# The third block's query load moved ahead of eight weight copies, and an order of its own for the last second-layer steps

## The chip, the cores and the metric

The kernel runs on one core of a Trainium2 chip. The metric is the device time of one execution in microseconds (us). Three runs of the kernel before gave 1104.61, 1104.78 and 1104.95 us; the median is 1104.78.

## The reference

Attention through 49 agents, then two feed-forward layers, on 12,480 tokens of width 128 with 2,048 hidden units, all in float32:

```python
a2k = sm(agents, k)            # softmax over the 12480 keys
agent_v = a2k @ v              # 49 x 128
q2a = sm(q, agents)            # softmax over the 49 agents
x = q2a @ agent_v              # 12480 x 128
h = x @ w_in                   # first layer
g = where(h >= 1, h, where(h <= -1, 0, (h + 1)**2 / 4));  x = g @ w_out
h = x @ w_in                   # second layer, own weights
g = s * max(h, 0)**2 + b;      out = g @ w_out
```

## The kernel before

**Tiling.** The tokens are cut into 25 blocks (`widths`, line 99): 256, then 23 times 512, then 448. A block goes through each layer in eight steps of 256 hidden units, so a layer has 200 steps, 0 to 199; steps 192 to 199 belong to the last block. Every float32 operand of the large products is held as a high and a low part, so a product takes several matmuls.

**One step.** In layer 1: the hidden product (`H`, lines 589 and 621, on PE), relu and square (`R`, `S`, ACT, lines 651 and 657), the cap (`M`, DVE, line 661), the high part `gh` (`c`, line 670 on ACT or 672 on DVE), the low part `gl` (`L`, DVE, line 677), and six output matmuls into the accumulator `y` (`O`, line 716), of which the third and the sixth need `gl`. In layer 2 the same without the cap, in small letters: `h` (line 602), `r`, `t`, `g` (tokens `G` and `C`), `l`, and `o` into the accumulator `o`. From step 189 on `g` is always on DVE. A finished `y` is split on ACT and DVE (`Y`, `y`, lines 735 and 738) before layer 2 can use it; a finished `o` is scaled by DVE into `osb` (`Z`, line 742) and stored. There is one `y` and one `o` buffer, and three `h` buffers.

**Prologue and ramp.** The prologue decodes the weights, forms the agents' values, and multiplies them into the first layer's weights (`awh`, `awl`). The ramp (`RAMP`, line 78) is a written list for steps 0 to 13. The token `q2` in it computes the scores of the third block's queries on PE (line 169), with its softmax in the tokens `z2.0` to `z2.9`. From the third block on layer 1 uses repacked weights `awm` and `awx` that `fill_rows` (line 607) copies from `awh` and `awl` with eight DMAs (lines 613, 614, 616).

**The DMA queue.** Every DMA is issued by SP, in the order of the program. The program gives the DMAs eight completion counters in turn, so that SP also waits, before a DMA, until the eighth one before it has landed. `load_q` (line 155) loads a block's queries into one of two buffers.

**The steady part.** `steady` (line 767) goes through the steps two at a time (`n0` = 14, 16, ...). Layer 2 runs 11 steps behind layer 1, and the output matmuls run two steps behind their `h`. For each `n0` the table `PAIR` (line 88) says in which order each engine takes its tokens; tokens that have no work any more are left out. From `n0` = 200 on layer 1 has only `O` of steps 198 and 199, the low part of step 199 and the split of the last `y` left; the rest is layer 2's steps from 187 to 199. Each engine works strictly through its own list.

Of the kernel before, what the change touches and what calls it, by code (L numbers as in the profile page):

```python
# [18 lines left out]
def kernel(  # L19
# [40 lines left out]

    SEQ = (
# [12 lines left out]
        "v11 v12 D1 q1"  # L76
    )
    RAMP = (
# [9 lines left out]
    PAIR = {  # L88
        "PE": "H0 h0 O0 o0 q0 O1 p1 p0 h1 q1 o1".split(),
        "ACT": "t0 P0 Y0 R0 R1 Q0 S0 S1 G0 r0 P1 Y1 t1 r1 Q1 G1".split(),  # L90
        "DVE": "L0 y0 C0 C1 Z1 F0 M0 M1 l0 Z0 c0 y1 c1 L1 l1 F1".split(),
    }
    QS, QT, DX = 7, 5, 1
    MASK_H = 0x7FFFFE00
# [60 lines left out]
    def load_q(t):  # L155
        if t >= NB:
            return
        t0, w = blocks[t]
        q_t[t] = qp.tile([P, TB], F32, tag="q", name=f"q{t}")
        nc.sync.dma_start(out=q_t[t][:, :w], in_=qT[:, t0:t0 + w])  # L160
# [162 lines left out]
    def prologue():  # L323
        with ExitStack() as pctx:
            pro = pctx.enter_context(tc.tile_pool(name="pro", bufs=1))
            dec = pctx.enter_context(tc.tile_pool(name="dec", bufs=1))
            wi1h = pro.tile([P, DFF], F32R, name="wi1h")
            wi1l = pro.tile([P, DFF], F32R, name="wi1l")
            agents_values(pro, dec, wi1h, wi1l)

    def agents_values(pro, dec, wi1h, wi1l):
# [239 lines left out]
        steps = {p: decode(dec, *pieces[p[0]], p) for p in WORD}  # L571
        for token in SEQ.split():
            kind, _, arg = token.partition(".")
# [9 lines left out]
    NS = NB * JP  # L583
# [23 lines left out]
    def fill_rows():  # L607

        extra["m"] = late.tile([P, DFF], F32R, name="awm")
        extra["x"] = late.tile([P, DFF // 4], F32R, name="awx")  # L610
        m, x, h, l = (w.bitcast(F32) for w in (extra["m"], extra["x"], awh, awl))
        for i, r in enumerate((0, LO)):
            nc.sync.dma_start(out=m[r:r + NA], in_=h[r:r + NA])
            nc.sync.dma_start(out=m[r + NA:r + NA + X1], in_=l[i * X1:(i + 1) * X1])
        for g in range(P // RG):
            nc.sync.dma_start(  # L616
                out=x[g * RG:g * RG + XL].rearrange("p (q m) -> p q m", m=P),
                in_=l[XN:NA].rearrange("p (q g m) -> p q g m", g=4, m=P)[:, :, g, :],
            )
# [64 lines left out]
    def GH(layer, n):  # L684
        if layer == 1:
            return PAT1[n] if n < len(PAT1) else "0"
        return PAT2[n % len(PAT2)] if n < NS - TL else "0"
# [79 lines left out]
    def steady():  # L767
# [20 lines left out]
            fillers.extend(later.pop(0))  # L788

        for n0 in range(NR, NS + D + D2 + 2, 2):  # L790
            for e, tokens in PAIR.items():
                for token in tokens:
                    c, n = token[0], n0 + int(token[1])
                    m, j, t = n - D, n % JP, n // JP
                    a, b = n < NS, 0 <= m < NS

                    def slot(key):

                        slots.append(key)
                        return [slots[-4]] if len(slots) > 3 else []  # L800

                    def add(key, deps, fn, *args):
                        lists[e].append((key, deps, fn, args))

                    if c == "H" and a and n == n0:
                        add(("H", n), slot(("M", n)) + slot(("M", n + 1)), first, n)
                    elif c == "O" and n - 2 < NS:
                        k = n - 2
                        add(("O", k), [("L", k), ("y", k // JP - 1)], O, 1, k)
                    elif c == "h" and b:  # L810
                        add(("h", m), slot(("r", m)) + [("y", m // JP)], H, 2, m)
                    elif c == "o" and 0 <= m - 2 < NS:
                        k = m - 2
                        add(("o", k), [("l", k), ("Z", k // JP - 1)], O, 2, k)
                    elif c == "q" and j == QS and t + 2 < NB:
                        add(("q", t + 2), slot(("Q", t + 2)), scores, t + 2)
                    elif c == "p" and t > 1 and j == QT and t + 1 < NB:
                        add(("p", t + 1), slot(("P", t + 1)) + [("F", n - 1, 1), ("Q", t + 1)], q_transpose, t + 1)
                    elif c == "Q" and j == QS and t + 2 < NB:
                        add(("Q", t + 2), [("q", t + 2)], scores_copy)  # L820
                    elif c == "P" and t > 1 and j == QT and t + 1 < NB:
                        add(("P", t + 1), [("p", t + 1)], q_evac)
                    elif c == "R" and a:
                        add(("R", n), [("H", n), ("H", n - 1), ("L", n - XB)], relu, 1, n)
                    elif c == "S" and a:
                        add(("S", n), [("R", n)], square, 1, n)
                    elif c == "M" and a:
                        add(("M", n), [("S", n)], cap, n)
                    elif c == "c" and a:
                        add(("c", n), [("M", n), ("O", n - GR)], hi, 1, n, False)  # L830
                    elif c == "L" and n - 1 < NS:
                        add(("L", n - 1), [("c", n - 1), ("O", n - 1 - GR)], lo, 1, n - 1)
                    elif c == "r" and 0 <= m < NS - 1:
                        add(("r", m), [("h", m), ("l", m - XB)], relu, 2, m)
                    elif c == "r" and m == NS - 1:
                        add(("r", m), [("h", m), ("l", m - XB), ("o", m - GR)], last_step, True)
                    elif c == "t" and 0 <= m - 1 < NS - 1:
                        add(("t", m - 1), [("r", m - 1)], square, 2, m - 1)
                    elif c in "GC" and 0 <= m - 1 < NS - 1 and (c == "G") == (GH(2, m - 1) == "1"):
                        add(("g", m - 1), [("t", m - 1), ("o", m - 1 - GR)], hi, 2, m - 1, c == "G")  # L840
                    elif c == "l" and 0 <= m - 1 < NS - 1:
                        add(("l", m - 1), [("g", m - 1), ("o", m - 1 - GR)], lo, 2, m - 1)
                    elif c == "l" and m - 1 == NS - 1:
                        add(("l", m - 1), [("r", m - 1)], last_step, False)
                    elif c == "Y" and (n - 2) % JP == JP - 1 and n - 2 < NS:
                        add(("Y", (n - 2) // JP), [("O", n - 2)], evac, 1, "h")
                    elif c == "y" and (n - 2) % JP == JP - 1 and n - 2 < NS:
                        add(("y", (n - 2) // JP), [("Y", (n - 2) // JP)], evac, 1, "l")
                    elif c == "Z" and 0 <= m - 2 < NS and (m - 2) % JP == JP - 1:
                        add(("Z", (m - 2) // JP), [("o", m - 2)], evac, 2, "")  # L850
                    elif c == "F":
                        for x in range(2):
                            add(("F", n, x), [], fill)
# [10 lines left out]
    with tc.manual_schedule():  # L864
        prologue()
        late = ctx.enter_context(tc.tile_pool(name="late", bufs=1))
        fill_rows()
        ramp()
        fillers.append(lambda: nc.vector.tensor_scalar_mul(bcol, bcol, b_sb[:, 0:1]))
        steady()  # L870
# [35 lines left out]
```

## Time and profile before

| | |
|---|---|
| median of three runs | 1104.78 us (1104.61 to 1104.95) |
| profiled execution | 1106.68 us, of which the span of the profile is 1104.9 us |
| PE busy | 1072.0 us, 97% of the span |
| ACT busy | 969.9 us, 88% |
| DVE busy | 964.8 us, 87% |
| chain that ended last | PE 89%, DVE 5%, ACT 2%, DMA 1%, SP's queue 1% |

PE is the tensor engine's matmul side, DVE the vector engine, ACT the scalar engine, SPq the queue of SP. Busy shares are means over stages with different limits; the chain names what each moment waited for.

### The profile page before, as it was taken

To read this page: it belongs to the slowest core of one execution; us is meant where nothing else is said; L and a number is where in the kernel's file an instruction comes from. 1 tells how busy PE (TensorE), PEld (TensorE's weight loads), DVE (VectorE), ACT (ScalarE), POOL (GpSimd) and SP (SyncE) were. 2 spreads that over 40 slices of the span, in tenths; PEclk is the share of its full clock that TensorE was granted. 3 is DMA by queue.
4 is the path that set the end of the run, shared out by engine and by line. 5 is a ranking of instruction groups with operands and counts; after the bars stand their busy time and mean duration, and the time that the engine had idled before them with its cause. 6 is when DMAs were issued, how large, how long until landed. Compare 5 with 4: busy or idle time off the path is not lost.

```text
span 1104.9 us, 13492 instructions
## 1 busy us (share of the span) xinstructions
PE 1072.0 (97%) x5050; PEld 823.4 (75%) x5050; DVE 964.8 (87%) x1194; ACT 969.9 (88%) x1132; POOL 0.8 (0%) x7
## 2 busy tenths in 40 slices
PE   6887999999999999999999999999999999999997
PEld 2676777777777777777777777777777777777776
DVE  8887889889889889889889889889889889889875
ACT  6876899889889889889889989989989989989974
POOL 0000000000000000000000000000000000000000
PEclk9898999999999999999999999999999999999999
DMA  9920000000000000000000000000000000000000
GB/s 351 394 79 23 19 23 24 4 28 24 4 28 25 3 28 25 3 27 26 3 27 26 3 27 26 2 27 27 1 28 27 1 27 27 1 18 18 1 10 18
DMA packets 19973, 41.01 MB, mean 37 GB/s; under 512 B 2638, under 2 KB 7976, under 8 KB 19268
## 3 DMA queue, kind: packets, MB, share of 16 engines
q1 hardware_dynamic: 19908, 40.15, 10.6%
q8 instruction: 40, 0.66, 0.3%
q14 instruction: 25, 0.20, 0.1%
HBM read 27.58 MB, written 6.39 MB: 31 GB/s over the span
## 4 chain that ended last, share of the span: by engine, by line
PE 89%; DVE 5%; ACT 2%; DMA 1%; SPq 1%; issue 1%; DVEq 0%
PE h L602 26%; PE o L716 24%; PE y L716 23%; PE h L632 7%; PE h L638 4%; PE qs L169 2%; DVE gl L677 1%; DMA k<-in_kT 1%; DVE x L661 1%; PE tp L212 1%; PE av L457 1%; ACT x L657 1%; SPq L616 1%; DVE gh L672 1%; DVE mxs L414 1%
## 5 line engine op out<-in xcount | busy, mean ns | idle before, releaser
L677 DVE TENSOR_TENSOR gl<-x,gh 128x1024 fp32r<-128x1024 f32 (+2 forms) x399 | 469.4, 1193 | 20.0 <-ACT gh L670 19.8
L657 ACT ACTIVATE x<-x 128x1024 f32<-128x1024 f32 (+2 forms) x399 | 404.4, 1043 | 1.9
L661 DVE SCALAR_TENSOR_TENSOR x<-h,x 128x1024 f32<-128x1024 f32 (+2 forms) x200 | 230.5, 1192 | 77.0 <-ACT x L657 76.4
L653 ACT ACTIVATE x<-h 128x1024 f32<-128x1024 f32 (+2 forms) x199 | 201.3, 1012 | 59.6 <-PE h L602 59.6
L651 ACT ACTIVATE x<-h 128x1024 f32<-128x1024 f32 (+2 forms) x200 | 190.0, 1005 | 2.9 <-DVE gl L677 1.0
L672 DVE CAST gh<-x 128x1024 fp32r<-128x1024 f32 (+2 forms) x251 | 164.0, 678 | 15.4 <-ACT x L657 15.2
L602 PE MATMUL h<-yh,wi2h 128*128 128x512 f32 (+2 forms) x400 | 166.7, 417 | 0.9 <-DVE x L661 0.9
L716 PE MATMUL o<-gl,wo2h 128*128 128x512 f32 (+2 forms) x400 | 157.9, 395 | 5.2 <-DVE gl L677 5.2
L716 PE MATMUL o<-gh,wo2h 128*128 128x512 f32 (+2 forms) x400 | 157.7, 394 | 1.9 <-DVE osb L742 1.8
L716 PE MATMUL y<-gl,wo1h 128*128 128x512 f32 (+2 forms) x400 | 156.6, 391 | 1.3 <-DVE gl L677 1.3
L716 PE MATMUL y<-gh,wo1h 128*128 128x512 f32 (+2 forms) x400 | 156.2, 391 | 0.1
L716 PE MATMUL y<-gh,wo1l 128*128 128x512 f32 (+2 forms) x400 | 156.2, 390 | 0.0
L716 PE MATMUL o<-gh,wo2l 128*128 128x512 f32 (+2 forms) x400 | 155.6, 389 | 0.0
L602 PE MATMUL h<-yh,wi2l 128*128 128x512 f32 (+2 forms) x400 | 155.5, 389 | 0.0
L602 PE MATMUL h<-yl,wi2h 128*128 128x512 f32 (+2 forms) x400 | 155.4, 389 | 0.0
L670 ACT ACTIVATE gh<-x 128x1024 fp32r<-128x1024 f32 (+1 forms) x148 | 152.2, 1030 | 0.9 <-DVE x L661 0.8
L602 PEld LDWEIGHTS h<-yh,wi2h 128*128 128x128 f32 x400 | 75.0, 187 | 36.7 <-issue 17.0
L632 PE MATMUL h<-pt,awm 128*128 128x512 f32 (+1 forms) x368 | 99.2, 391 | 0.0
L716 PEld LDWEIGHTS o<-gl,wo2h 128*128 128x128 f32 x400 | 75.0, 188 | 28.3 <-DVE gl L677 12.2
L716 PEld LDWEIGHTS y<-gl,wo1h 128*128 128x128 f32 x400 | 75.6, 189 | 19.7 <-DVE gl L677 2.8
L716 PEld LDWEIGHTS o<-gh,wo2h 128*128 128x128 f32 x400 | 75.2, 188 | 18.8 <-DVE osb L742 2.1
L716 PEld LDWEIGHTS y<-gh,wo1h 128*128 128x128 f32 x400 | 75.6, 189 | 17.3 <-ACT gh L670 0.3
(114 smaller groups left out, 909.8 us busy)
## 6 DMA issues: line engine op xcount, KB each, us to landing
k<-in_kT SPq DMA_DIRECT2D x12, 512.0 KB, 12.7
v<-in_v_main SPq DMA_DIRECT2D x12, 512.0 KB, 8.5
q<-in_qT SPq DMA_DIRECT2D x23, 256.0 KB, 4.9
out_T<-osb SPq DMA_DIRECT2D x23, 256.0 KB, 2.1
wu<-in_w_in SPq DMA_DIRECT2D x4, 1024.0 KB
px<-pt SPq DMA_DIRECT2D x88, 38.0 KB
wu<-in_w_out SPq DMA_DIRECT2D x3, 1024.0 KB
pt<-pt SPq DMA_DIRECT2D x44, 30.0 KB
```

What stands on the lines that cost most here:

```text
L169: nc.tensor.matmul(out=scv[:, i, :], lhsT=qt[:, c0:c0 + P], rhs=aT, start=True, stop=True)
L602: nc.tensor.matmul(out=h[:, i, :w], lhsT=a[:, sl], rhs=r, start=(m == 0), stop=(m == len(ops) - 1))
L632: nc.tensor.matmul(out=out[g], lhsT=awm[:, c * P:(c + 1) * P], rhs=pt_t[t][:, :w], start=True, stop=False)
L638: nc.tensor.matmul(out=out[g], lhsT=awx[r, q], rhs=px_t[t][r, :w], start=False, stop=True)
L651: nc.scalar.activation(out=x, in_=h, func=ACTF.Relu, scale=0.5, bias=0.5)
L653: nc.scalar.activation(out=x, in_=h, func=ACTF.Relu)
L657: nc.scalar.activation(out=x, in_=x, func=ACTF.Square)
L661: nc.vector.scalar_tensor_tensor(out=x, in0=h, scalar=1.0, in1=x, op0=ALU.max, op1=ALU.min)
L670: nc.scalar.activation(out=a, in_=x, func=ACTF.Copy)
L672: nc.vector.tensor_copy(out=a, in_=x)
L677: nc.vector.tensor_tensor(out=b, in0=x, in1=a.bitcast(F32), op=ALU.subtract)
L716: nc.tensor.matmul(out=o[:, :w], lhsT=l[:, c, :], rhs=r[:, i, :w], start=(c == 0 and m == 0), stop=(c == KF - 1 and m == 2),)
```

## The change

The diff, without the unchanged parts of the tables:

```diff
     RAMP = (
-        "u2 H0 q1 R0 H1 S0 z1.0 M0 R1 z1.1 H2 g0 ...
+        "H0 q1 R0 H1 S0 z1.0 M0 R1 z1.1 H2 g0 ...
...
+    TAIL = {
+        "PE": "H0 O0 h0 o0 O1 h1 o1".split(),
+        "ACT": "Y0 R0 S0 t0 G0 r0 Y1 R1 S1 t1 G1 r1 P0 P1 Q0 Q1".split(),
+        "DVE": "C0 l0 L0 M0 y0 Z0 c0 F0 C1 l1 L1 M1 y1 Z1 c1 F1".split(),
+    }
...
         for n0 in range(NR, NS + D + D2 + 2, 2):
-            for e, tokens in PAIR.items():
+            for e, tokens in (PAIR if n0 < NS else TAIL).items():
...
         late = ctx.enter_context(tc.tile_pool(name="late", bufs=1))
+        load_q(2)
         fill_rows()
         ramp()
```

The token `u2` was `load_q(2)`. It stood first in the ramp, behind the eight copies of `fill_rows`; it now stands in front of them. The number of instructions on each engine stays the same. Lines below the table move down by six or seven.

On SP, at the end of the prologue, the rows before (the names carry the tile's number and a running number; `q2` is the third block's queries):

```order
L256 DMA wu_486<-in_w_in2 128x2048
L160 DMA q1_488<-in_qT 128x512
L384 DMA s_sb_76<-in_s 128x1
L385 DMA b_sb_77<-in_b 128x1
L613 DMA awm_660<-awh_80 49x2048
L614 DMA awm_660<-awl_81 15x2048
L613 DMA awm_660<-awh_80 49x2048
L614 DMA awm_660<-awl_81 15x2048
L616 DMA awx_661<-awl_81 19x4x128 x4
L160 DMA q2_670<-in_qT 128x512
L160 DMA q3_845<-in_qT 128x512
```

And the same place on SP now:

```order
L262 DMA wu_486<-in_w_in2 128x2048
L166 DMA q1_488<-in_qT 128x512
L390 DMA s_sb_76<-in_s 128x1
L391 DMA b_sb_77<-in_b 128x1
L166 DMA q2_660<-in_qT 128x512
L619 DMA awm_662<-awh_80 49x2048
L620 DMA awm_662<-awl_81 15x2048
L619 DMA awm_662<-awh_80 49x2048
L620 DMA awm_662<-awl_81 15x2048
L622 DMA awx_663<-awl_81 19x4x128 x4
L166 DMA q3_845<-in_qT 128x512
```

The load of `q2` passed the eight copies; its counter's earlier DMA is now a load of values (the eighth before it) instead of the first copy.

On DVE, at `n0` = 200 and 202, before (`gl2_188` is the low part of layer 2's step 188, `gl1_199` that of layer 1's step 199, `yl24` the low part of the last `y`):

```order
L677 TENSOR_TENSOR gl1_199_9259<-x1_199_9205,gh1_199_9218 128x2x448
L672 CAST gh2_189_9287<-x2_189_9255 128x1024
L677 TENSOR_TENSOR gl2_188_9289<-x2_188_9248,gh2_188_9253 128x1024
L738 TENSOR_TENSOR yl24_9281<-y24_9024,yh24_9280 128x448
L677 TENSOR_TENSOR gl2_189_9292<-x2_189_9255,gh2_189_9287 128x1024
L672 CAST gh2_190_9294<-x2_190_9284 128x1024
L672 CAST gh2_191_9328<-x2_191_9322 128x1024
L677 TENSOR_TENSOR gl2_190_9330<-x2_190_9284,gh2_190_9294 128x1024
L677 TENSOR_TENSOR gl2_191_9332<-x2_191_9322,gh2_191_9328 128x1024
```

The same place on DVE now:

```order
L683 TENSOR_TENSOR gl2_188_9259<-x2_188_9248,gh2_188_9253 128x1024
L683 TENSOR_TENSOR gl1_199_9261<-x1_199_9205,gh1_199_9218 128x2x448
L678 CAST gh2_189_9305<-x2_189_9255 128x1024
L683 TENSOR_TENSOR gl2_189_9307<-x2_189_9255,gh2_189_9305 128x1024
L744 TENSOR_TENSOR yl24_9296<-y24_9024,yh24_9295 128x448
L678 CAST gh2_190_9310<-x2_190_9299 128x1024
L683 TENSOR_TENSOR gl2_190_9312<-x2_190_9299,gh2_190_9310 128x1024
L678 CAST gh2_191_9314<-x2_191_9302 128x1024
L683 TENSOR_TENSOR gl2_191_9316<-x2_191_9302,gh2_191_9314 128x1024
```

The low part of step 188 no longer stands behind the cast of step 189, but ahead of the low part of layer 1's step 199; in every later pair each low part follows its own cast.

On DVE, at `n0` = 204, where `osb23` frees the one `o` buffer for the last block, before:

```order
L672 CAST gh2_192_9334<-x2_192_9325 128x2x448
L672 CAST gh2_193_9368<-x2_193_9362 128x2x448
L677 TENSOR_TENSOR gl2_192_9370<-x2_192_9325,gh2_192_9334 128x2x448
L742 TENSOR_SCALAR osb23_9372<-o23_9161,s_sb_76,bcol_78 128x512
L677 TENSOR_TENSOR gl2_193_9375<-x2_193_9362,gh2_193_9368 128x2x448
```

And now:

```order
L678 CAST gh2_192_9366<-x2_192_9357 128x2x448
L683 TENSOR_TENSOR gl2_192_9368<-x2_192_9357,gh2_192_9366 128x2x448
L748 TENSOR_SCALAR osb23_9370<-o23_9161,s_sb_76,bcol_78 128x512
L678 CAST gh2_193_9373<-x2_193_9360 128x2x448
L683 TENSOR_TENSOR gl2_193_9375<-x2_193_9360,gh2_193_9373 128x2x448
```

`osb23` no longer stands behind the cast of step 193. On PE one thing moves: the six `O` matmuls of step 198 stand ahead of the six `h` matmuls of step 189 instead of behind them. ACT's order is the same.

## Rows read from the trace of the kernel before

**Rows 1.** The page's first line
```profile
span 1104.9 us, 13492 instructions
```
**Rows 2.** Busy time by window: start:end, length, busy of each engine, PE clock, DMA
```profile
136.00:1056.00 920.00, 919.89 (x4201) 708.88 (x4202) 826.20 (x979) 840.71 (x940) 0.00 (x0) 1.00 0.06 18
```
**Rows 3.** Waits of PE, whole span: total us, times, longest
```profile
PE qs L169 <- DMA q<-in_qT: 6.5, 2, 5.1
PE o L716 <- DVE gl L677: 5.2, 6, 1.6
PE o L716 <- DVE osb L742: 1.8, 1, 1.8
```
**Rows 4.** Timeline, SP's queue, and the first use of awm: start, us
```profile
54.64 0.43 SPq L385 DMA_DIRECT2D b_sb<-in_b  x1
...
69.66 0.90 SPq L613 DMA_DIRECT2D awm<-awh  x1
...
82.34 2.07 SPq L160 DMA_DIRECT2D q<-in_qT  x2
...
117.98 1.09 PE L632 MATMUL h<-pt,awm 128*128 128x512 f32 x4
```
**Rows 5.** Timeline of the ramp around the q2 scores; idle before and its releaser bracketed
```profile
83.04 0.28 PE L716 MATMUL y<-gl,wo1h 128*128 128x256 f32 x1
...
83.74 1.28 DVE L677 TENSOR_TENSOR gl<-x,gh 128x512 fp32r<-128x512 f32 x2
...
88.44 1.78 PE L169 MATMUL qs<-a,q 128*128 128x49 f32 x8 [5.12 <-DMA q<-in_qT]
...
90.62 0.36 DVE L186 TENSOR_REDUCE qm<-qe 128x4 f32<-128x196 f32 x1 [5.60 <-ACT qe L176]
...
91.57 1.23 DVE L661 SCALAR_TENSOR_TENSOR x<-h,x 128x1024 f32<-128x1024 f32 x1 [0.19 <-ACT x L657]
...
94.66 0.38 ACT L735 ACTIVATE yh<-y 128x256 fp32r<-128x256 f32 x1 [1.54 <-PE y L716]
...
95.07 0.42 DVE L738 TENSOR_TENSOR yl<-y,yh 128x256 fp32r<-128x256 f32 x1 [1.55 <-ACT yh L735]
```
**Rows 6.** Busy time by window in the ramp: PE, PEld, DVE, ACT, POOL, then clock
```profile
88.40:95.00 6.60, 6.56 (x26) 6.11 (x27) 2.64 (x4) 2.65 (x5) 0.00 (x0) 0.51 0.01 3
96.00:108.00 12.00, 11.51 (x60) 9.21 (x60) 12.00 (x18) 11.85 (x16) 0.00 (x0) 1.00 0.00 0
```
**Rows 7.** Chain of waits near the end: six matmuls each, start, us
```profile
1060.51 1.40 PE h L602 x6
1061.91 1.21 PE y L716 x6
```
**Rows 8.** Timeline of the tail
```profile
1060.35 0.39 PE L602 MATMUL h<-yh,wi2h 128*128 128x512 f32 x1
...
1061.15 2.23 DVE L677 TENSOR_TENSOR gl<-x,gh 128x1024 fp32r<-128x1024 f32 x2 [0.93 <-ACT gh L670]
...
1062.10 1.06 ACT L670 ACTIVATE gh<-x 128x1024 fp32r<-128x1024 f32 x1
...
1065.78 0.54 ACT L735 ACTIVATE yh<-y 128x448 fp32r<-128x448 f32 x1 [1.70 <-PE y L716]
...
1067.30 0.69 DVE L672 CAST gh<-x 128x1024 fp32r<-128x1024 f32 x1 [3.92 <-ACT x L657]
...
1081.78 0.81 DVE L742 TENSOR_SCALAR osb<-o,s_sb,bcol 128x512 f32<-128x512 f32 x1
...
1082.63 0.47 PE L716 MATMUL o<-gh,wo2h 128*128 128x448 f32 x1 [1.76 <-DVE osb L742]
...
1085.37 0.92 ACT L653 ACTIVATE x<-h 128x896 f32<-128x896 f32 x1 [2.56 <-PE h L602]
...
1087.84 2.08 DVE L677 TENSOR_TENSOR gl<-x,gh 128x896 fp32r<-128x896 f32 x2
...
1100.59 0.47 PE L716 MATMUL o<-gl,wo2h 128*128 128x448 f32 x1
```

2 rows, old and new, of the table RAMP are left out of this document.

## The prediction

> **What bounds the kernel now.** I read the page first, then the busy time by window, then PE's waits over the whole span, and last the timelines around the places where PE waits. From 136 to 1056 us PE is busy for 919.89 of 920.00 us at a granted clock of 1.00 [rows 2]: in the steady part PE is the bound and nothing else can be late. So a gain there must come from fewer matmuls, and the change has the same ones. What is left is outside: PE's list of waits [rows 3] holds 6.5 us for a load of queries, of which one wait is 5.1 us, 5.2 us in output matmuls for a low part `gl`, and 1.8 us for the `o` buffer. The timelines place the 5.1 us in the ramp [rows 5], and the 1.8 us and nearly all of the 5.2 us in the tail, behind 1061 us [rows 8]. These are the two places that the change touches. A microsecond won in the ramp moves the whole PE-bound part forward, so it stays won; the two gains add.
>
> **The ramp: the load of q2.** Before, SP issues the load at 82.34, behind eight copies of which the first could only start at 69.66, when the multiplied weights were ready [rows 4]. PE begins its last matmul in front of the scores at 83.04, stands idle for 5.12 us, and begins the scores at 88.44 [rows 5]. Now the load stands right behind the load of `b_sb`, which SP issues at 54.64 [rows 4]. It has to wait for one earlier load of values to land, by its counter; the two buffers are no obstacle, as the first block's scores are long done. From 82.34 to 88.4 it took about 6 us from issue to use, so the queries lie there around 61 to 66 us, 17 us or more before PE wants them at 83.2. The wait on the load goes entirely.
>
> What is late next? I walk the three engines from 83 us, with the durations of the rows.
>
> PE begins the scores at about 83.15. They took 1.78 us at a granted clock of 0.51 [rows 5, 6], the 1.2 GHz level, so about 0.9 us at 2.4 GHz. Then come four hidden matmuls of 512 columns and twelve output matmuls of 256. Six of 512 columns take 1.40 us at full clock [rows 7], 0.233 each, and I take half of it for 256: 0.93 and 1.40 us. PE is done with `y` of the first block at 83.15 + 0.9 + 0.93 + 1.40 = 86.4. ACT can take `yh` 0.2 us later if it is free. Between 88.4 and 95.0 ACT does 2.65 us of work, the end of `yh` included [rows 6]; started at 84.3, behind the first score matmuls' end, it ends `yh` at 86.95. Before, `yh` began at 94.66 [rows 5].
>
> DVE ends its work at 83.74 + 1.28 = 85.02 [rows 5]. Then it idles three times before 95.07: 5.60 us for the scores, 0.19 us for a square that ACT could only do behind the scores' copy, and 1.55 us for `yh` [rows 5]. All three hang on the late scores. Its work in this stretch is 2.64 us [rows 6]: without the idle time it reaches the split of `y` at 85.02 + 2.64 = 87.7, when `yh` (86.95) is there. So DVE is now the last of the three: its idle time of 5.60 + 0.19 + 1.55 = 7.3 us is what the ramp can give. From 96 to 108 us DVE is busy for 12.00 of 12.00 us [rows 6], so that it can't make up more, though PE and ACT arrive some 8.0 us earlier; they wait for DVE instead. I take 7.3 us. Ends of the range: 5.1 us if only PE's idle time goes and something else holds the rest, 8.0 us if PE's arrival decides (94.66 less 86.6).
>
> The part of this above the plain wait is the clock. PE did 6.56 us of work at 0.51 after its stop [rows 6]. The Trainium skill, "TensorE: Matmul & The Clock Gate", section "HAM oscillation — how this bites in real kernels", prices a stretch at the low clock at half its length. By that rule 3.3 us come back and, with a stop of 5.3 us, PE alone would win 8.6 us; the trace agrees that the clock halves, but its full DVE at 96 to 108 us leaves no room for the sum.
>
> The eight copies lose nothing: SP waited for the weights until 69.66 anyway, and has been done with the load for some 5 us or more. Their first user stands at 117.98 [rows 4], now 110.7, and before the copies had all been issued at 82.34. The load's 256 KB come behind the last weights in the same queue; I price a disturbance of the prologue at 0 to 0.6 us and take nothing.
>
> **The tail.** First what PE has to do. From 1060.35 to the end stand 26 groups of six matmuls: 8 of 512 columns (`h` 189 to 191, `o` 187 to 191) at 1.40 us and 18 of 448 (`O` 198 and 199, `h` 192 to 199, `o` 192 to 199) at 1.21 to 1.22 [rows 7]: 11.2 + 21.9 = 33.1 us. The last matmul begins at 1100.59 [rows 8] and holds PE 0.2 us: 40.4 us went by. So PE loses 7.3 us there, the idle time of the rows and the slower restart behind each stop.
>
> Why it loses them: DVE's cast of step 189 stood ahead of the low part of step 188. It waited 3.92 us, until 1067.30 [rows 8], for a square that stood on ACT behind `Y` of the last block (1065.78), while ACT's high part of step 188 had been done at 1062.10 + 1.06 = 1063.16. In each later pair the first low part stood behind the second cast in the same way, and `osb23` too: it began at 1081.78 and PE waited for it until 1082.63 [rows 8].
>
> Now, with the times of before the ramp's shift: `O` 198 and `h` 189 change places, 1060.35 + 1.21 + 1.40 = 1062.96; `o` 187 to 1064.36; `O` 199 begins. DVE does the low part of 187 at 1061.15, then waits for 1063.16, then does the low part of 188 until about 1064.3, and only then that of layer 1's step 199, until 1065.4 (two took 2.23 us [rows 8]). The third matmul of `O` 199 was due at 1064.77 and begins at 1065.45. That is a new wait; with the restart it costs 0.8 us. Its followers: `Y` at 1066.5, ACT's square of 189 until 1068.0, cast and low part of 189 until 1069.8, split of `y` until 1070.4. PE meanwhile: `O` 199 to 1066.4, `h` 190 to 1067.8, `o` 188 to 1069.2 without a stop, `h` 191 to 1070.6, `o` 189, whose third matmul wants the low part at 1071.0: there. `h` 192 to 1073.2, `o` 190 to 1074.6, `h` 193 to 1075.8, `o` 191 to 1077.2. `osb23` runs from 1077.4 for 0.81 us, to 1078.2; PE does `h` 194 until 1078.4 and begins `o` 192 then, against 1082.63 before. The margin is 0.2 us, the smallest of the walk. From there on a step needs, from its relu to its low part's end, 1085.37 to 1087.84 + 1.04, 3.5 us [rows 8], while PE has four groups, 4.9 us, between an `h` and its `o`: PE no longer stops. The last step's own halves are unchanged and I leave 0.1 us of the loss to them. The tail wins 7.3 - 0.8 - 0.1 = 6.4 us. Ends: 7.3 us if the new wait is hidden; 4.6 us if a wait as long as that for `osb23`, 1.8 us, stays.
>
> **The sum.** 7.3 + 6.4 = 13.7 us off the span of 1104.9 [rows 1], 1091.2, and the profiled execution of 1106.68 would be 1093.0. That execution lies 1.9 us above the median of the runs; against the median the forecast is 1104.78 - 13.7 = 1091.1 us.
>
> **Rivals.**
> *PE's arrival decides in the ramp* (what the page's rule above points to): 8.0 us there, 1090.4. For it speaks that DVE's full window has some short pieces of the softmax that may move; against it the 12.00 of 12.00. Chance 0.10.
> *Only the plain wait goes*: the clock falls in another short stop of the new ramp, or another engine holds PE: 5.1 + 6.4, 1093.3. Against it: the walk has no PE stop above 0.7 us. Chance 0.10.
> *The tail keeps a wait*: `osb23` misses its margin or `Y` is later than I think: 7.3 + 4.6, 1092.9. Chance 0.08.
> *The load moves but does not come early*, because SP still holds it until the weights are ready: the ramp gives nothing, 1098.4. Against it: its counter's earlier DMA is now a load of values. Chance 0.05. *The new order gives nothing in the tail*, each wait being replaced: 1097.5, chance 0.03.
> *Slower*: SP is one queue, so whatever holds the load now holds the eight copies too. Their user stands at 110.7 and they end before 88.4, so a delay below about 22 us is hidden; to lose the tail's 6.4 us and 2.2 us more SP would have to stand for 31 us past 69.66. I see nothing that could hold it so long. It would be 1107 us or more; chance 0.02.
> No change at all needs both halves to fail: 0.02.
>
> **How the numbers follow.** The forecast has the remaining 0.60, with a range of its own of 1089.8 to 1092.5. The range is 1089.3 to 1095.5: below, both upper ends (8.0 + 7.3 = 15.3, 1089.5) and a little; above, the two weaker cases and both lower ends (5.1 + 4.6 = 9.7, 1095.1). About 0.88 of the chance stands in these cases; I leave the rest for what I don't see. A measurement tells no change from one of 0.2%, 2.2 us. All cases but the last two are faster by more: 0.96; within 0.2%: 0.02; slower: 0.02.
>
> **What the new profile would show.** The load of q2 issued below 62 us and no wait of PE on queries but the first block's; a PE clock near 1.00 from 83 to 95 us; the split of the first `y` on DVE near 87.7 and the first matmul on `awm` near 110.7. In the tail one wait of PE for a low part, in `y`, below 1 us near 1057.5 (1064.8 less 7.3); `o` 192 beginning near 1071; none for `osb`; the last matmul near 1086.9. If the first `awm` matmul comes earlier by clearly less than 7 us, the ramp's term is wrong; if the way from it to the end shrinks by clearly less than 6 us, the tail's.

## The result and the profile after

The changed kernel took 1090.74 us, the median of four runs (1090.12 to 1091.85). The kernel before took 1104.87 us in four runs beside it (1104.61 to 1106.73). The ratio is 0.987, with a 95% interval of 0.9853 to 0.9887: 14.1 us less, where the forecast was 1091.1 and 13.7.

The page's first line, in answer to [rows 1]:

```profile
span 1088.3 us, 13497 instructions
```

The busy time by window, in answer to [rows 2] and [rows 6] (start:end, length, busy of PE, PEld, DVE, ACT, POOL, then PE's clock):

```profile
83.00:90.00 7.00, 6.29 (x33) 4.51 (x32) 6.97 (x11) 6.79 (x10) 0.00 (x0) 1.00 0.09 30
90.00:96.00 6.00, 5.99 (x28) 4.71 (x29) 6.00 (x10) 5.71 (x9) 0.00 (x0) 1.00 0.00 0
...
129.00:1042.00 913.00, 912.89 (x4169) 703.49 (x4167) 819.90 (x970) 834.17 (x932) 0.00 (x0) 1.00 0.06 18
```

The steady part is as full as before. In the ramp the clock is 1.00 where it was 0.51, and it is now DVE that has no gap there (12.97 of 13.00 us, PE 12.28). PE's waits over the whole span, in answer to [rows 3]:

```profile
PE y L722 <- DVE gl L683: 2.1, 6, 0.5
...
PE qs L175 <- DMA q<-in_qT: 1.4, 1, 1.4
...
PE o L722 <- DVE gl L683: 0.9, 2, 0.5
```

The 5.1 us for `q2` and the 1.8 us for `osb` are gone, and the 5.2 us in `o` have become 0.9. Those 0.9 stand outside the tail; the 1.4 us that are left for queries are the first block's. SP's queue, in answer to [rows 4]:

```profile
53.57 0.33 SPq L391 DMA_DIRECT2D b_sb<-in_b  x1
54.89 0.33 SPq L166 DMA_DIRECT2D q<-in_qT  x1
67.29 0.91 SPq L619 DMA_DIRECT2D awm<-awh  x1
...
80.50 1.28 SPq L166 DMA_DIRECT2D q<-in_qT  x1
```

The second row is the load of `q2`, 12 us ahead of the first copy; the last is the load of `q3`, issued 13.2 us behind the first copy (before, 82.34 - 69.66 = 12.7). PE's timeline in the ramp and around the last steps, in answer to [rows 5] and [rows 8]:

```profile
80.72 0.98 PE L175 MATMUL qs<-a,q 128*128 128x49 f32 x8
...
83.95 0.39 PE L608 MATMUL h<-pt,awh 128*128 128x512 f32 x1
...
107.90 1.09 PE L638 MATMUL h<-pt,awm 128*128 128x512 f32 x4
...
1041.72 0.47 PE L644 MATMUL h<-px,awx 19*128 19x448 f32 x4
...
1055.38 0.47 PE L722 MATMUL y<-gl,wo1h 128*128 128x448 f32 x1 [0.54 <-DVE gl L683]
...
1068.33 0.37 PE L722 MATMUL o<-gh,wo2h 128*128 128x448 f32 x1
...
1084.05 0.47 PE L722 MATMUL o<-gl,wo2h 128*128 128x448 f32 x1
```

The scores begin without a stop and take 0.98 instead of 1.78 us. In the tail there is the one wait in `y` that was foretold, and `o192` (1068.33) begins straight behind an `h`. DVE at the same places:

```profile
81.29 1.29 DVE L683 TENSOR_TENSOR gl<-x,gh 128x512 fp32r<-128x512 f32 x2
82.49 0.35 DVE L192 TENSOR_REDUCE qm<-qe 128x4 f32<-128x196 f32 x1
82.88 0.36 DVE L193 TENSOR_TENSOR qe<-qe,qm 128x196 f32<-128x196 f32 x1
83.16 1.22 DVE L667 SCALAR_TENSOR_TENSOR x<-h,x 128x1024 f32<-128x1024 f32 x1
84.41 0.69 DVE L678 CAST gh<-x 128x1024 fp32r<-128x1024 f32 x1
85.02 0.42 DVE L744 TENSOR_TENSOR yl<-y,yh 128x256 fp32r<-128x256 f32 x1
...
1053.10 2.23 DVE L683 TENSOR_TENSOR gl<-x,gh 128x1024 fp32r<-128x1024 f32 x2 [0.81 <-ACT gh L676]
1058.01 0.69 DVE L678 CAST gh<-x 128x1024 fp32r<-128x1024 f32 x1 [2.69 <-ACT x L663]
...
1067.32 0.81 DVE L748 TENSOR_SCALAR osb<-o,s_sb,bcol 128x512 f32<-128x512 f32 x1 [0.25 <-PE o L722]
```

None of the three idle times of [rows 5] is left between 81.29 and 85.02. In the tail the two low parts of the first pair stand in front of the cast that waits, and `osb` ends at 1068.13, 0.2 us before `o192`.

The split at 85.02 also needs ACT's high part of that `y`, which was done at 84.54:

```profile
84.15 0.39 ACT L741 ACTIVATE yh<-y 128x256 fp32r<-128x256 f32 x1 [0.21 <-PE y L722]
```

To see where the time came from I cut each trace at four starts: the first `awm` copy on SP, the first `awm` matmul, the last `awx` matmul, and the last matmul of all. For the change that is 67.29, 107.90, 1041.72 and 1084.05; for the kernel before 69.66, 117.98 [rows 4], 1051.82 and 1100.59 [rows 8]. Before, the last `awx` group:

```profile
1051.82 0.47 PE L638 MATMUL h<-px,awx 19*128 19x448 f32 x4
```

In the table, ramp, middle and tail are the three distances between these starts, in us. The last column is the granted clock of 40 to 50 us, in the prologue.

| kernel | first copy | ramp | middle | tail | clock 40–50 |
|---|---|---|---|---|---|
| before | 69.66 | 48.32 | 933.84 | 48.77 | 0.79 |
| changed | 67.29 | 40.61 | 933.82 | 42.33 | 0.94 |
| a0_changed_again | 68.74 | 40.59 | 933.57 | 42.33 | 0.81 |
| e1_load_only | 68.60 | 40.59 | 933.85 | 48.78 | 0.86 |
| e2_tail_only | 68.03 | 48.60 | 933.89 | 42.35 | 0.90 |

The ramp gave 7.7 us and the tail 6.4; together 14.1, as the timed runs say. The profiles stand 16.5 us apart at the last matmul (1100.59 to 1084.05), because the first copy was 2.4 us earlier too. That part isn't the change's: the changed kernel run again (1091.16 us, 1090.05 to 1092.34; ratio 0.9873, interval 0.9859 to 0.9888) has its copy at 68.74 with the same ramp and tail, and `e6_first_pair` below, with the same early load, has it at 69.68.

### The profile page after: what moved, and what is told of

Its sections match the earlier page's. It is cut to its first block, busy times and chain, and to the rows that moved or that the text cites. A ratio compares the mean times of both kernels' runs of the same rounds, so it can differ in the third digit from the quotient of the medians.

```text
span 1088.3 us, 13497 instructions
## 1 busy us (share of the span) xinstructions
PE 1065.8 (98%) x5050; PEld 818.1 (75%) x5050; DVE 965.5 (89%) x1194; ACT 970.2 (89%) x1132; POOL 0.9 (0%) x7
## 4 chain that ended last, share of the span: by engine, by line
PE 90%; DVE 6%; ACT 2%; DMA 1%; issue 1%; SPq 0%; DVEq 0%; ACTq 0%
PE h L608 26%; PE o L722 25%; PE y L722 23%; PE h L638 8%; PE h L644 4%; PE qs L175 2%; DVE x L667 1%; DVE gl L683 1%; DMA k<-in_kT 1%; PE tp L218 1%; PE av L463 1%; DVE mxs L420 1%; ACT x L657 1%; DVE gh L678 1%; DVE wt L305 0%
## 5 line engine op out<-in xcount | busy, mean ns | idle before, releaser
L722 PEld LDWEIGHTS y<-gh,wo1l 128*128 128x128 f32 x400 | 75.1, 188 | 17.0
```

The source lines that it names most:

```text
L722: nc.tensor.matmul(out=o[:, :w], lhsT=l[:, c, :], rhs=r[:, i, :w], start=(c == 0 and m == 0), stop=(c == KF - 1 and m == 2),)
```

## The experiments

**Each half alone.** Two kernels, each the changed one with one half undone:

```diff
# e1_load_only
-            for e, tokens in (PAIR if n0 < NS else TAIL).items():
+            for e, tokens in PAIR.items():
# e2_tail_only
-        "H0 q1 R0 H1 S0 ...
+        "u2 H0 q1 R0 H1 S0 ...
-        load_q(2)
         fill_rows()
```

> Only the load of q2 is moved; the tail keeps the old table. Theory (the two parts add, each as read from the two traces): from the first copy of awm to the first matmul on awm 40.6 us as in the changed kernel (48.3 before), from h 189's first matmul to the last matmul 40.2 us as before; 1097.2 us, 7.7 less than before. Rival (the parts feed each other, the tail's waits change when the ramp is earlier): the tail is not 40.2 us and the time is more than 1 us off 1097.2.

> Only the tail's table; the load of q2 stays behind the copies. Theory (additive): 48.3 us from the first copy to the first matmul on awm as before, with the wait of 5.1 us for the queries, and the tail shorter by 6.4 us: 1098.4 us. Rival (the parts feed each other): off that by more than 1 us.

Measured: 1097.93 us for the load (1097.42 to 1098.72; ratio 0.9934, 0.9919 to 0.9949) and 1099.23 for the tail (1098.36 to 1099.67; ratio 0.9945, 0.9928 to 0.9961). The table shows each half at its full size alone, and the other place as before: the gains add.

**How much of the ramp is the clock.** The kernel before, with PE kept busy in its stop in front of the scores by twenty matmuls whose results nobody reads:

```diff
# e4_late_warm, against before
-        "M7 g6 q2 u3 R8 ...
+        "M7 g6 w q2 u3 R8 ...
+        def keep_warm():
+            idle = ps_o("idle2")
+            for i in range(DUM):      # 20
+                nc.tensor.matmul(out=idle, lhsT=wi2h[:, 0:P], rhs=wi2h[:, 0:TB], start=True, stop=True)
```

> The kernel before with 20 extra matmuls of 512 columns on PE, on data long there, in front of the q2 scores, so that PE is busy while it waits for the late queries. The wait for the load stays; the low clock behind it should go. Theory (DVE decides): DVE keeps its 5.6 us of idle time for the scores and loses the 1.55 us for yh, so from the first copy to the first matmul on awm 46.8 us (48.3 before), 1103.3 us. Rival 1 (PE's arrival decides): all of the clock's 2.7 us come back, 45.6 us and 1102.2 us. Rival 2 (the clock costs nothing because DVE has slack): 48.3 us and no change.

PE's timeline, then DVE's, then the windows of that kernel:

```profile
82.80 4.71 PE L756 MATMUL idle<-wi2h 128*128 128x512 f32 x20
88.36 1.06 PE L170 MATMUL qs<-a,q 128*128 128x49 f32 x8 [0.85 <-DMA q<-in_qT]
...
91.63 0.39 PE L603 MATMUL h<-pt,awh 128*128 128x512 f32 x1
```
```profile
89.83 0.36 DVE L187 TENSOR_REDUCE qm<-qe 128x4 f32<-128x196 f32 x1 [5.17 <-ACT qe L177]
...
92.64 0.42 DVE L739 TENSOR_TENSOR yl<-y,yh 128x256 fp32r<-128x256 f32 x1
```
```profile
82.00:96.00 14.00, 13.02 (x71) 10.43 (x70) 8.46 (x14) 8.04 (x12) 0.00 (x0) 1.00 0.16 46
...
1082.00:1086.00 4.00, 4.00 (x14) 3.54 (x14) 0.24 (x1) 1.87 (x2) 0.00 (x0) 0.61 0.00 0
```

Measured: 1103.61 us (1102.45 to 1105.13; ratio 0.9984, 0.9974 to 0.9993), ramp 46.16 us. That is 2.16 less than before, and lies between the two numbers expected. Counted from each kernel's first copy, DVE's `yl` came 2.16 us earlier (92.64 - 69.39 against 95.07 - 69.66), PE's next `h` matmul 2.52 (91.63 - 69.39 against 94.42 - 69.66). So what DVE won is what the ramp won, to 0.01 us, and PE's extra was lost. My 46.8 missed that the scores at full clock also reach DVE sooner: its wait for them is 5.17 here, 5.60 before. Of the change's 7.7 us, about 2.2 are thus the clock and, by difference, 5.5 the load. The scores began 0.19 us later against the first copy than before (88.36 - 69.39 against 88.44 - 69.66), so the clock's part may be up to 0.2 us more. The tail of this kernel was 49.67, 0.9 longer than before's: the clock fell to 0.61 behind the `osb` stop of 1.76 us, though nothing had been changed there. I come back to that.

**Which engine decides in the ramp.** The changed kernel with 0.46 us more for PE (two matmuls read by nobody), and with 1.2 us more for DVE (the low part of step 8 written twice), both behind the split of the first `y`:

```diff
# e9_more_pe: keep_warm as above, with 2 matmuls
-   ... S9 y H11 L8 R10 ...
+   ... S9 y H11 w L8 R10 ...
# e10_more_dve
+   ... S9 y H11 L8 w8 R10 ...
+        def again(n):
+            x, a, b = (gv(g, 1, n) for g in (gx, gh, gl))
+            nc.vector.tensor_tensor(out=b, in0=x, in1=a.bitcast(F32), op=ALU.subtract)
```

> The changed kernel with two extra matmuls of 512 columns on PE in the ramp, in front of O 8 (0.47 us of PE work, read by nobody). Theory (DVE decides the ramp from the scores on and PE waits for it): from the first copy to the first matmul on awm 40.6 us as before the addition, within 0.1. Rival (PE's arrival decides): 41.1 us.

> The changed kernel with one DVE instruction of the ramp done twice: the low part of layer 1's step 8 (1.14 us from start to start). Theory (DVE decides the ramp): the whole of it comes on top, 41.7 us from the first copy to the first matmul on awm. Rival (PE's arrival decides and DVE has slack): 40.6 to 41.0 us.

PE of the first kernel, then DVE of the second:

```profile
85.86 0.62 PE L761 MATMUL idle<-wi2h 128*128 128x512 f32 x2
86.32 0.39 PE L722 MATMUL y<-gh,wo1h 128*128 128x512 f32 x1
```
```profile
87.01 1.22 DVE L683 TENSOR_TENSOR gl<-x,gh 128x1024 fp32r<-128x1024 f32 x1
88.26 1.23 DVE L760 TENSOR_TENSOR gl<-x,gh 128x1024 fp32r<-128x1024 f32 x1
89.40 1.22 DVE L667 SCALAR_TENSOR_TENSOR x<-h,x 128x1024 f32<-128x1024 f32 x1
```

With more for PE the ramp was 40.62 us, 0.01 from the change's 40.61 (one time: 1090.3). With more for DVE it was 41.86, 1.25 more (one time: 1093.18). DVE decides; PE has the 0.46 us to spare at this place. "One time" here and below is a single execution, so that the reading rests on its trace and not on its time.

**Where the load has to stand.** The load between the copies into `awm` and those into `awx`:

```diff
# e5_load_middle: in fill_rows, between its two loops; none in front of it
+        load_q(2)
```

> The changed kernel with the load of q2 between the four copies of awm and the four of awx, so that it is issued about 5 us behind the first copy instead of 12 us ahead of it. Theory (only the moment at which the queries lie there counts; 6 us from issue to use): they lie there some 11.5 us behind the first copy, the scores are wanted about 13.5 us behind it, so no wait and the same time as the changed kernel, 40.6 us from the first copy to the first matmul on awm. Rival (the transfer shares the DMA engines with the copies and is late): PE waits for the queries again, up to 2 us.

```profile
68.15 0.91 SPq L619 DMA_DIRECT2D awm<-awh  x1
...
73.40 1.90 SPq L166 DMA_DIRECT2D q<-in_qT  x1
75.35 6.76 SPq L623 DMA_DIRECT2D awx<-awl  x4
```

Issued at 73.40 instead of 54.89, it cost nothing: ramp 40.58, 1091.14 us (1089.99 to 1091.62). Only that the queries lie there in time counts.

**The tail by pairs.** The new order in the later pairs alone, and in the first pair alone:

```diff
# e7_later_pairs
-  (PAIR if n0 < NS else TAIL)
+  (PAIR if n0 < NS + 2 else TAIL)
# e6_first_pair
+  (TAIL if n0 == NS else PAIR)
```

> The changed kernel with the old table for n0 = 200 and the new one from 202 on. Theory: the wait for the low part of step 188 comes back (1.6 us, 1.85 with the restart) and the new wait in y (0.8) goes; all later waits stay away: about 34.9 us from h 189 to the last matmul (40.2 before), one wait of o, none for osb. Rival: with l 188 late, the margin of osb23 is lost too and PE waits a second time.

> The changed kernel with the new table at n0 = 200 only and the old one from 202 on. Theory (the tail's waits add up one by one): the wait for l 188 goes, the one in y comes (0.8), and the later waits, two casts ahead of the first low part and osb23 behind both, stay: from the last matmul on awx to the last matmul 48.8 - 1.05 = 47.7 us, against 42.3 with the whole table. Rival (repairing the first pair lets the later ones catch up): below 46.5 us.

The later pairs alone have a tail of 43.38 us (one time: 1091.6): 5.4 of the 6.4 us. From `h` 189 to the last matmul it took 34.84 us, where 34.9 were expected, with one wait in the tail, in `o`:

```profile
1059.53 0.50 PE L722 MATMUL o<-gl,wo2h 128*128 128x512 f32 x1 [1.58 <-DVE gl L683]
```

The first pair alone missed what was expected: 48.84 us, no gain (one time: 1098.98), though its waits on DVE were shorter. Its PE windows and timeline show why:

```profile
1060.00:1073.80 13.80, 11.10 (x49) 8.75 (x47) 8.91 (x12) 9.79 (x11) 0.00 (x0) 1.00 0.00 0
1073.80:1077.00 3.20, 3.14 (x11) 2.87 (x12) 1.54 (x3) 0.23 (x1) 0.00 (x0) 0.71 0.22 82
1077.00:1081.00 4.00, 3.95 (x16) 3.22 (x15) 1.40 (x2) 2.29 (x3) 0.00 (x0) 0.80 0.00 0
```
```profile
1073.86 0.47 PE L722 MATMUL o<-gh,wo2h 128*128 128x448 f32 x1 [1.76 <-DVE osb L748]
...
1075.18 0.57 PE L608 MATMUL h<-yh,wi2h 128*128 128x448 f32 x1
...
1077.42 0.57 PE L722 MATMUL o<-gh,wo2h 128*128 128x448 f32 x1
```

Behind the `osb` wait the clock fell, so that an `h` group took 2.24 us (1075.18 to 1077.42) instead of 1.21 [rows 7]. Before has the same wait, 1.76 us [rows 8], and kept its clock at 1.00; this is its window behind the wait:

```profile
1082.60:1086.00 3.40, 3.37 (x17) 3.13 (x18) 1.52 (x2) 0.84 (x2) 0.00 (x0) 1.00 0.21 77
```

To see whether this took the gain, PE did six idle matmuls inside that wait:

```diff
# e11_warm_wait, against e6_first_pair; in O, ahead of o_ps[layer] = ...
+            if layer == 2 and t == NB - 1:
+                idle = ps_y("idle2")
+                for i in range(6):
+                    nc.tensor.matmul(out=idle, lhsT=wi2h[:, 0:P], rhs=wi2h[:, 0:TB], start=True, stop=True)
```

> As the kernel with the new order in the first pair of the tail alone (e6_first_pair), and PE does six idle matmuls of 512 columns (1.4 us at full clock, results read by nobody) in front of o192, inside its wait for osb. e6 gained nothing in the tail (48.84 us from the last awx matmul to the last matmul, as the 48.77 of before) although its waits were 1.6 us shorter; behind its osb wait of 1.76 us the clock stood at 0.71 and 0.80 for 7 us, where before had 1.00. Theory: that low clock ate the gain. With PE busy in the wait the clock stays near 1.00 from 1072 to 1094, and the tail is 47.7 to 47.9 us: ramp as in the change, 1097.8 in time. Rival: the clock is not what ate it (or does not depend on this wait): the tail stays at 48.6 to 48.9, 1098.9, and the clock dips all the same or later waits take the gain.

```profile
1070.69 1.55 PE L719 MATMUL idle<-wi2h 128*128 128x512 f32 x6
1072.62 0.47 PE L726 MATMUL o<-gh,wo2h 128*128 128x448 f32 x1 [0.37 <-DVE osb L752]
```
```profile
1072.00:1078.00 6.00, 5.63 (x28) 4.80 (x26) 2.81 (x5) 2.89 (x4) 0.00 (x0) 1.00 0.12 44
```

The clock stayed at 1.00 and the tail was 47.77 us (1042.81 to 1090.58), 1.07 less: the expected gain of the first pair, back. Timed: 1096.5 us (1095.88 to 1096.66; ratio 0.992, 0.9903 to 0.9937).

**The new wait in `y`.** Two kernels that let the low part of layer 1's step 199 go first; the second also puts ACT's square of 189 ahead of the copy of `y`:

```diff
# e3_first_low (both)
-        "DVE": "C0 l0 L0 M0 y0 ...
+        "DVE": "C0 L0 l0 M0 y0 ...
# e8_low_and_square also
-        "ACT": "Y0 R0 S0 t0 G0 r0 Y1 ...
+        "ACT": "t0 G0 r0 R0 S0 Y0 R1 S1 t1 Y1 G1 r1 ...
```

> The changed kernel, but at n0 = 200 DVE takes the low part of layer 1's step 199 ahead of that of layer 2's step 188. Theory (the new wait of PE in y is the price of that order and nothing else waits for l 188 so early): the wait of 0.54 us in y goes, Y starts about 0.8 us earlier, o 188 still finds its low part, the tail is 0.7 to 0.8 us shorter and the time about 1090.0 us. Rival: the wait only moves to o 188, no change.

> As the kernel before this one, and ACT takes the square of step 189 ahead of Y of the last block. Theory (PE waits for nothing behind O 199): no more than e3_first_low, within 0.2 us of it in the trace. Rival (the late square is still on the path): another few tenths less.

Both tails are 41.53 us, 0.80 less than the change's. PE in the first of them, at the group that waited:

```profile
1055.59 0.37 PE L722 MATMUL y<-gh,wo1l 128*128 128x448 f32 x1
1055.80 0.36 PE L722 MATMUL y<-gl,wo1h 128*128 128x448 f32 x1
```

So the wait cost its 0.8 us, and moving the square adds nothing. Timed they were 1090.5 (1089.7 to 1091.63; ratio 0.9868, 0.9853 to 0.9883) and 1090.62 (1089.07 to 1091.57; ratio 0.9867, 0.9852 to 0.9882), beside 1091.16 for the change on the same chip: the intervals overlap, so that the 0.8 us is shown by the trace alone. Theirs is the shortest tail of all versions.

## Why the prediction was right, step by step

**The load comes early and PE's wait goes: right.** It was issued at 54.89 (foretold: below 62), and PE waits for no queries but the first block's. The eight copies lost nothing that PE saw: the load behind them was issued at 80.50, 27 us ahead of their first user at 107.90, though SP got to it 0.5 us later behind the first copy than before.

**DVE is the last of three: right.** The walk put the split of the first `y` at 87.7 in before's time; it stands at 85.02. The changed kernel's first copy came 2.37 us earlier (67.29 against 69.66); with these added, which is what "before's time" means below, it stands at 87.39. PE's next `h` (83.95) is 86.32 in that time, 8.1 us earlier than before's 94.42; this is the arrival that the first rival would have paid out as 8.0. The ramp paid 7.7, which is DVE's 95.07 - 87.39. That lies as near to the rival's 8.0 as to the forecast's 7.3, so the size alone doesn't tell the two apart; e9 and e10 do, each side by itself. ACT's `yh` was foretold to end at 86.95, ahead of the split, and ended at 86.91 in before's time (84.54 + 2.37).

**The size of the ramp's term: 7.3 forecast, 7.7 measured.** The walk laid DVE's work end to end behind 85.02, with the 2.64 us of [rows 6]. In the new trace an instruction that nothing holds begins before the row of the one ahead has ended: the reduction at 82.49 while the low parts' row runs to 82.58, the cap at 83.16 before 83.24, the split at 85.02 before 85.10. The scores' first instruction comes at 84.86 in before's time and the split 2.53 us later, which makes 87.39. A stop hides such overlaps, so idle time summed over stops undercounts slightly: the overlaps come to 0.25 us of the 0.4 that were missing. Another 0.08 is that the low parts themselves begin earlier against the first copy (81.29 + 2.37 = 83.66, before 83.74). The Trainium skill, "VectorE: DVE Perf Modes", section "The DRAIN you can't avoid", says that a next operation that is not held starts earlier than the emptying of the pipe would let it, without a figure; the rows agree in kind, with 0.08 to 0.09 us at each of these three places.

**The clock's part: right in kind.** PE did 6.56 us at 0.51 [rows 6], and the ramp got 2.2 us for it in e4. By the price of the Trainium skill, "TensorE: Matmul & The Clock Gate", section "HAM oscillation — how this bites in real kernels", half the stretch, the estimate would be 3.3. PE itself won less than that: from its first score to the `h` behind `y` it took 3.27 us in e4 (91.63 - 88.36) and 5.98 before (94.42 - 88.44), 2.7 less. Of these 0.19 went to the later start of the scores, and 0.36 was lost because DVE comes last, which is the reason that the prediction gave.

**The tail: 6.4 forecast, 6.44 measured.** The one new wait costs 0.8 us, as e3 shows by removing it. One reading of the prediction was off without touching this sum: of the 5.2 us that PE waited for low parts in `o`, 4.2 stood in the tail, not nearly all; the other 1.0 stood at 127.07 and 135.89 and is still there (0.9). The two low parts run in one piece behind `gh` (1053.10), no `osb` wait is left, and the margin there is the 0.2 us of the walk. In before's time `o192` begins at 1070.7 and the last matmul at 1086.4; foretold were 1071 and 1086.9, and the 0.4 us between are the ramp's. The later pairs carry 5.4 us of it, the first pair 1.05.

**What I had not asked.** The forecast let PE keep its clock behind every stop of the old tail, as the one trace of before did. The tail of e1, which has the old order, did so too (1.00, 48.78 us). e4, again with that order, and e6 show that this isn't sure: their falls cost 0.9 and 1.1 us. Where an execution of the kernel before pays such a fall, the change gains that as well, since it has no such stop; how often that is, these runs don't tell.

## What to carry to other kernels

When a stop goes, walk every engine from it to the next place where one of them has no gap, and take the gain of the one that comes last, not of the one that stood still: here PE was 8.1 us earlier and the kernel got DVE's 7.7. A transfer has only to be there in time, so move it just past what it stood behind (12.4 us ahead of the first copy and 5.3 us behind it were all one). In a tail that drains, let each engine's list follow one step to its end before it starts waiting for the next one, and let what is ready go ahead of what is not. The change breaks the second half once: DVE waits 0.81 us for a `gh` (at 1053.10) with the low part of layer 1's step 199, ready by then, behind it in the list; e3 turns the two round and wins 0.8 us.

## What the runs showed of the hardware that I had not expected

The prologue's length changes from run to run, and the granted clock with it, in kernels that have the same work there, up to the place of one load. Before, then the change:

```profile
40.00:50.00 10.00, 10.00 (x102) 8.41 (x101) 5.95 (x10) 7.50 (x16) 0.00 (x0) 0.79 1.03 409
```
```profile
40.00:50.00 10.00, 9.86 (x122) 7.87 (x122) 7.25 (x14) 9.20 (x20) 0.00 (x0) 0.94 1.03 410
```

At 0.94 PE got 122 matmuls done in these 10 us, at 0.79 it got 102, and the first copy came 2.4 us sooner. The changed kernel itself, run again, had 0.81 and its copy at 68.74, so the change isn't the reason. Over the other kernels the two go together in the same way, for instance 68.03 with 0.90, 68.60 with 0.86, 69.39 with 0.80 and 69.68 with 0.78. That the clock makes the length, and not something behind both, no run shows. Two profiles should therefore be cut at a common event, as in the table, before their spans are compared.

The second is the stop of 1.76 us for `osb`: the clock stayed at 1.00 behind it in before and in e1, and fell to 0.61 in e4 and to 0.71 and 0.80 in e6. With PE busy in it (e11), it did not fall. What tells the two cases apart stays open.
